# Later attention rounds in groups of 32 queries: block transposes on VectorE and small transfers in place of TensorE transposes

## The chip, the cores and the metric

The kernel runs on one core of a Trainium2 chip. The metric is device time in microseconds (us) of one execution, the median over runs. Engines are named as the profile names them: PE is TensorE (PEld its weight loads), DVE VectorE, ACT ScalarE, POOL GpSimd, SP SyncE, which here only issues transfers (DMA).

## The reference

Causal attention over 4 batches, 8 heads, 576 positions of 64 numbers, then a dense MLP on 2304 tokens, then a top-1 mixture of eight experts, all in float32:

```
rel = pos[:, None] - pos[None, :]
mask_local   = (rel >= 0) & (rel < 32)                       # heads 0..3
mask_strided = (rel >= 0) & (pos[None, :] % 32 == pos[:, None] % 32)   # heads 4..7
scores = where(mask, q @ k.T / 8, -1e9);  scores -= scores.max(-1)
attn = exp(scores); attn = attn / (attn.sum(-1) + 1e-9);  x = attn @ v       # (2304, 512)
r = maximum(x @ w_in, 0);  x = (s * r * r + b) @ w_out       # 512 -> 2048 -> 512
e = argmax(x @ w_gate)     # the token's expert: out = gate * relu(x @ w1[e]) @ w2[e]
```

## The kernel before

A local head's query sees the 32 keys up to itself, a strided head's query only keys of its own position modulo 32, so attention is done in small rounds and never as a 576 x 576 product. `GROUPS` lists the rounds as (kind, batch, first block, number n of blocks). A block of a local round ("L") is 64 consecutive queries against 96 keys. A strided head's keys of one residue are a class; a block of a strided round ("P", "U", "T") holds several classes side by side, "P" and "U" the first positions of a batch, "T" the rest of them, with 72 or 90 keys in a "T" block. Every round does its blocks for four heads at once: two heads in the two halves of the 128 partitions of q and k, and two more (index p) in the two halves of the output's partitions.

The MLP's two layers follow: `first_layer` (L918) and `second_layer` (L952) each issue twelve matmuls per step (three passes of four), for units of 256 or 512 tokens, and between them ACT squares the hidden values and splits them in two parts (L866, L878, L890), DVE takes the second part (L892). A unit's first layer needs the attention output of its tokens.

The order on every engine is written ahead by a planner, the class `Order`: each piece of work is a generator that yields (engine, cost, what it waits for), and the planner gives each engine the piece that can start first by its own estimates. What it gives is static: an engine does its instructions in that order and waits where one is not ready. The first nine rounds (`NEARLY`) run before the MLP and are not touched. The 21 later ones are spread over the MLP's steps; `PACE` names the step before which a round's scores may not stand.

A late round does this, by line: scores on PE into two banks (L585), mask added on DVE (L602), maximum (L611), difference (L625), exponential on ACT (L629), sum (L631), reciprocal (L633, L634), product (L636), all on DVE; PE transposes the probabilities by identity matmuls into PSUM (L656), ACT or DVE copies them to the buffer `ph` (L662, L664); PE multiplies with the values (L695, the PV step); ACT and DVE write the result in two parts into the MLP's input `xsl` (L734, L751). q with k, and v, come by one load each on SP's queue (L538).

Of the kernel before, what the change touches and what calls it, by code (L numbers as in the profile page):

```python
# [43 lines left out]
NEG = -8589934592.0  # L44
NQV = 2
NG = 2
# [5 lines left out]
NPR = 2  # L52
NPH = 1
NQE = 6
# [18 lines left out]
P_ATT1 = -0.1  # L73
P_ATT2 = -0.02
XLO_PE = ()
EXPB = (0, 1, 3, 4, 5, 6, 7, 8)
MASKV = range(9, 30)
# [13 lines left out]
def steps():  # L91
# [11 lines left out]


def part_of(g):

    kind, b = GROUPS[g][0:2]
    late = kind == "T"
    return FIRST[b] * late, CLS if late else FIRST[b], RES[b][late]


def dims(g):

    if GROUPS[g][0] == "L":
        return QB, LK
    j0, j1, r = part_of(g)
    return r * (j1 - j0), QB if GROUPS[g][0] == "P" else r * j1

# [9 lines left out]
def residues(g, i):  # L128
    r = part_of(g)[2]
    return range((GROUPS[g][2] + i) * r, min(STRIDE, (GROUPS[g][2] + i + 1) * r))  # L130
# [176 lines left out]
def body(ctx, tc, qkv, w12, moe_s, moe_b, wg, e12, out):  # L307
# [24 lines left out]
    m_loc0, m_loc = mk[:, 0:LK], mk[:, LK:2 * LK]  # L332
    xm = at.tile([P, max(sum(x) for x in MB[1:])], F32R, name="xm", tag="xm", bufs=1)
    mh = wp.tile([P, sum(MB[0])], F32R, name="mh", tag="w")
# [152 lines left out]
    ev_mp = Ev()  # L487
    ev_md = [Ev() for _ in range(B)]

    def masks(b, mf=None):  # L490
        if b == 0:
            yield op(("POOL", 3.0))
            make_masks(0, (1,), mf[:, 2 * LK:])
            nc.gpsimd.memset(wgt, 0.0)
            nc.gpsimd.iota(wt, pattern=[[-1, E]], base=E, channel_multiplier=0, allow_small_or_imprecise_dtypes=True)
            yield op(("ACT", 0.3))
            nc.scalar.activation(out=mh[:, MB[0][0]:], in_=mf[:, 2 * LK + MB[0][0]:], func=AF.Copy)
            o.set(ev_mb[0])
# [5 lines left out]
        nc.scalar.activation(out=xm[:, 0:sum(MB[b])], in_=t[:, 0:sum(MB[b])], func=AF.Copy)
        o.set(ev_mb[b])
        if b + 1 < B:
            o.spawn(masks(b + 1))

# [19 lines left out]
    def load_qkv(at):  # L528
        g, k = LOADS[at]
        w = widths(g)[k]  # L530
        yield op(("DMA", 0.00128 * w + (1.2 if at == 2 else 0.0)), waits=([t_qe if g < NEARLY else t_qv] if k == 0 else []) + ([t_w] if g < NEARLY else []),
                 late=LATE_Q[at] if at < len(LATE_Q) else P_QKL)
        if g < NEARLY:
            t = wp.tile([P, w], F32, name="qkv", tag="w")
        else:
            t = at_pool.tile([P, (WQ, WV)[k]], F32, name="qkv", tag=("qk", "vv")[k], bufs=NQV)[:, 0:w]
        wq = widths(g)[0]
        nc.sync.dma_start(out=t, in_=qkv[g, k * P * wq:P * (wq + k * w)].rearrange("(p n) -> p n", n=w))  # L538
        qkvs[g, k] = t
        o.set(ev_qkv[g, k], o.fin + DMA_LAT)  # L540
        if at + 1 < len(LOADS):
            o.spawn(load_qkv(at + 1), after=False)

    def attn(g):
        kind, b, i0, n = GROUPS[g]
        strided = kind == "P"
        early = g < NEARLY
        qw, w = dims(g)
        m_g = mask_of(g)
        nk = P if strided else w  # L550
        local = kind == "L"
        pairs = pair_early if early else pair_late
        singles = t_att + t_l2 if early else t_att

        def buf(name):
            if early:
                return wp.tile([P, 1024], F32, name=name, tag="w"), t_w
            return at.tile([P, {"pr": 6 * LK, "ph": 6 * P}[name]], F32, name=name, tag=name, bufs={"pr": NPR, "ph": NPH}[name]), {"pr": t_pr, "ph": t_ph}[name]

        step = PACE.get(g, -1)  # L560
        pace = [ev_k[step]] if step >= 0 else []
        yield op(("PE", n * (0.24 + 0.0015 * w) + 0.1 - (0.45 if g in MASKV else 0)), waits=[pairs, ev_qkv[g, 0], ev_mk if local else ev_mp if g < NFIRST else ev_mb[b], t_sm, t_w if early else t_pr] + pace, dep=False)
        toks = o.got[0:2]
# [17 lines left out]
        for i in range(n):  # L581
            at_i = 2 * (i % (n // 2)) + i // (n // 2) if strided else i
            for p in range(2):
                for h in range(2):
                    nc.tensor.matmul(out=sc[p * QB:(p + 1) * QB, h, at_i, :], lhsT=q[h * D:(h + 1) * D, p, i * qs:i * qs + QB],  # L585
                                     rhs=k[h * D:(h + 1) * D, p, i * kstep:i * kstep + w], start=not by_pe, stop=not by_pe or i == n - 1)
        if by_pe and g == T_LAST[b]:
            if b == 0:
                o.free(t_w)
            o.set(ev_md[b])  # L590
        if g + 1 < len(GROUPS):
# [4 lines left out]
        bc = [x.rearrange("p (h i) -> p h i", h=2).unsqueeze(3).to_broadcast([P, 2, n, w]) for x in v]  # L596
        src = sc
        if not by_pe:
            yield op(("DVE", cols / 960 + 0.15), on=toks)
            for i, j, mask in [(0, 1, m_loc0)] * a + [(a, n, m_g)] * (a < n):  # L600
                mask = (mask if mask.dtype == F32 else mask.bitcast(F32)).unsqueeze(1).unsqueeze(1).to_broadcast([P, 2, j - i, w])
                nc.vector.tensor_tensor(out=pr[:, :, i:j, :], in0=sc[:, :, i:j, :], in1=mask, op=ALU.add)  # L602
            for tok in toks:
                o.free(tok)
            src = pr
            if g == T_LAST[b]:
                if b == 0:
                    o.free(t_w)
                o.set(ev_md[b])
        yield op(("DVE", cols / 960 + 0.16), on=toks if by_pe else [])  # L610
        nc.vector.tensor_reduce(out=v[0].rearrange("p (h i) -> p h i", h=2), in_=src, axis=AX.X, op=ALU.max)  # L611
        if g in EXPB:
# [62 lines left out]
        for i in range(n):  # L675
            if not nq[i]:
                continue
            for p in range(2):
                for h in range(2):
# [14 lines left out]
                    else:  # L694
                        nc.tensor.matmul(out=dst, lhsT=lhs, rhs=rhs)  # L695
        if early:
            o.free(t_qe)
            o.free(t_w)
            o.free(t_w)
        else:  # L700
            o.free(t_qv)
        o.free(ph_tok)
# [17 lines left out]
        for k, (tok, nn, src, dst, done) in enumerate(runs):  # L720
# [1205 lines left out]
```

## Time and profile before

| | |
|---|---|
| median of 3 runs | 698.48 us (696.97 to 700.14) |
| the profiled execution | 700.7 us, span 699.0 us |
| granted TensorE clock, mean over the span | 0.992 of full speed |
| busy share of PE, DVE, ACT, POOL | 98%, 52%, 43%, 4% |
| attention's instructions on PE from 75 to 377 us (scores, transposes, PV) | 400, 98, 400 records |

The span is the profiled execution from its first to its last instruction; the 1.7 us more are what lies around it. A share is busy time over the whole span and mixes stages; which engine sets the pace of a stage is read in windows of time.

### The profile page before, as it was taken

What the parts mean: (1) busy time and instruction counts of PE and PEld (TensorE: products, weight loads), DVE (VectorE), ACT (ScalarE), POOL (GpSimd) and SP (SyncE); (2) the same over time, 40 slices, a digit from 0 to 9 for tenths busy, and PEclk for the clock granted to TensorE, in tenths of its full rate; (3) what the DMA queues carried; (4) which work ended last, traced back from release to release, by engine and by line L of the source; (5) the groups of instructions that cost most, each with busy time, mean ns of one, the idle gap of its engine ahead of it and who ended that gap; (6) DMA issues with size and microseconds to landing.
All of it is one profiled execution on the core that took longest, in us unless ns stands there. A gap on an engine that the chain in (4) does not pass through costs nothing. (4 is left out here: it accounts for less than half of the span.)

```text
span 699.0 us, 11984 instructions
## 1 busy us (share of the span) xinstructions
PE 688.2 (98%) x4702; PEld 577.3 (83%) x4702; DVE 364.5 (52%) x856; ACT 301.7 (43%) x630; POOL 25.2 (4%) x100
## 2 busy tenths in 40 slices
PE   7999999999999999999999999999999999999996
PEld 6888877898778777878778878888899999998895
DVE  4798888855144343145333144443567854764340
ACT  4776654655353443353433354554431432323221
POOL 5000000032000000000000000001000000000000
PEclk9799999999999999999999999999999999999999
DMA  8983513242222113022110023110120271307101
GB/s 303 406 315 105 198 62 114 92 145 80 91 93 69 39 40 102 1 93 72 39 46 1 0 93 123 56 62 30 61 91 1 84 255 63 120 2 265 58 10 64
DMA packets 28109, 69.00 MB, mean 99 GB/s; under 512 B 4237, under 2 KB 7310, under 8 KB 27282
## 3 DMA queue, kind: packets, MB, share of 16 engines
q1 hardware_dynamic: 27922, 68.19, 28.0%
q8 instruction: 38, 0.62, 0.4%
q14 instruction: 21, 0.17, 0.1%
q0 software_dynamic: 128, 0.02, 0.0%
HBM read 56.75 MB, written 11.69 MB: 98 GB/s over the span
## 5 line engine op out<-in xcount | busy, mean ns | idle before, releaser
L918 PE MATMUL h<-xsl,w 128*128 128x512 f32 (+1 forms) x876 | 206.8, 381 | 0.0
L952 PE MATMUL bk<-g,w 128*128 128x512 f32 (+1 forms) x864 | 203.4, 381 | 0.0
L918 PEld LDWEIGHTS h<-xsl,w 128*128 128x128 f32 x876 | 155.6, 188 | 31.4 <-issue 0.8
L952 PEld LDWEIGHTS bk<-g,w 128*128 128x128 f32 x864 | 153.3, 188 | 31.6 <-issue 2.1
L866 ACT ACTIVATE r<-h 128x512 f32<-128x512 f32 (+1 forms) x80 | 44.5, 556 | 180.8 <-PE h L918 168.4
L892 DVE TENSOR_TENSOR g<-r,g 128x512 fp32r<-128x512 f32 (+1 forms) x73 | 48.1, 659 | 131.1 <-ACT g L890 130.6
L1423 PE MATMUL bk<-w,ht 128*128 128x512 f32 x384 | 96.8, 393 | 0.0
L1423 PEld LDWEIGHTS bk<-w,ht 128*128 128x128 f32 x384 | 68.6, 188 | 12.1
L890 ACT ACTIVATE g<-r 128x512 fp32r<-128x512 f32 (+1 forms) x73 | 44.2, 605 | 2.7
L878 ACT ACTIVATE r<-r 128x512 f32<-128x512 f32 (+1 forms) x72 | 43.8, 608 | 2.2
L1316 ACT ACTIVATE ht<-h 128x256 fp32r<-128x256 f32 x24 | 9.2, 385 | 74.3 <-PE h L1477 54.5
L695 PEld LDWEIGHTS bk<-ph,qkv 96*64 96x64 f32 (+4 forms) x608 | 20.7, 144 | 9.4 <-issue 6.7
L1477 PEld LDWEIGHTS h<-x,wa 128*128 128x128 f32 x192 | 26.4, 188 | 2.3 <-issue 0.4
L1477 PE MATMUL h<-x,wa 128*128 128x256 f32 x192 | 28.0, 281 | 0.0
L1477 PE MATMUL bk<-x,wc 128*128 128x256 f32 x192 | 27.8, 280 | 0.0
L1477 PE MATMUL h<-x,wc 128*128 128x256 f32 x192 | 27.7, 280 | 0.0
L1477 PEld LDWEIGHTS h<-x,wc 128*128 128x128 f32 x192 | 25.6, 188 | 1.3 <-DVE su L1354 0.3
L1477 PEld LDWEIGHTS bk<-x,wc 128*128 128x128 f32 x192 | 24.8, 188 | 0.2 <-issue 0.2
L695 PE MATMUL bk<-ph,qkv 96*64 96x64 f32 (+9 forms) x608 | 24.6, 233 | 0.1
L585 PEld LDWEIGHTS bk<-qkv 64*64 64x64 f32 x608 | 14.2, 141 | 11.9 <-issue 6.0
L662 ACT ACTIVATE ph<-bk 96x768 f32<-96x768 f32 (+10 forms) x27 | 18.4, 680 | 12.4 <-PE bk L656 11.6
L585 PE MATMUL bk<-qkv 64*64 64x96 f32 (+4 forms) x608 | 19.8, 258 | 3.5 <-DMA qkv<-qkv 3.5
(229 smaller groups left out, 761.5 us busy)
## 6 DMA issues: line engine op xcount, KB each, us to landing
raw<-w SPq DMA_DIRECT2D x32, 512.0 KB, 7.6
qkv<-qkv SPq DMA_DIRECT2D x14, 384.0 KB, 3.2
out<-ob SPq DMA_DIRECT2D x17, 256.0 KB, 2.0
xd<-x SPq DMA_DIRECT2D x4, 1024.0 KB, 4.2
wraw<-e SPq DMA_DIRECT2D x16, 256.0 KB, 2.7
xr<-xd SPq DMA_DIRECT2D x8, 512.0 KB, 5.0
X<-xd SPq DMA_DIRECT2D x4, 1024.0 KB, 10.2
we<-e SPq DMA_DIRECT2D x8, 512.0 KB, 6.7
```

What stands on the lines that cost most here:

```text
L585: nc.tensor.matmul(out=sc[p * QB:(p + 1) * QB, h, at_i, :], lhsT=q[h * D:(h + 1) * D, p, i * qs:i * qs + QB], rhs=k[h * D:(h + 1) * D, p, ...
L662: nc.scalar.activation(out=dst, in_=pt[0:nk], func=AF.Copy)
L695: nc.tensor.matmul(out=dst, lhsT=lhs, rhs=rhs)
L866: nc.scalar.activation(out=r, in_=h, func=AF.Relu)
L878: nc.scalar.activation(out=to, in_=r, func=AF.Square)
L890: nc.scalar.activation(out=gt[:, 0, 0:U], in_=r, func=AF.Copy)
L892: nc.vector.tensor_sub(out=gt[:, 1, 0:U], in0=r, in1=gt[:, 0, 0:U].bitcast(F32))
L918: nc.tensor.matmul(out=h, lhsT=w_t[2 * fc][:, a, c * P:(c + 1) * P], rhs=xt(u, c, x), start=(c == 0 and n == 0), stop=(c == KD - 1 and n = ...
L952: nc.tensor.matmul(out=acc[pu][c], lhsT=w_t[2 * pf + 1][:, a, c * P:(c + 1) * P], rhs=gt[:, x, 0:cols(pu)], start=(first and n == 0), stop ...
L1316: nc.scalar.activation(out=ht[:, 0, a:b], in_=src, func=AF.Relu)
L1423: nc.tensor.matmul(out=acc2[s, t][0], lhsT=box[k][:, x, t * P:(t + 1) * P], rhs=w_t["p", 2 * f + 1][:, a, :], start=(f == 0 and n == 0), s ...
L1477: nc.tensor.matmul(out=banks[to], lhsT=t[:, a, off + c * P:off + (c + 1) * P], rhs=x2[s, b][:, y, c, :], start=(first and c == 0 and n == ...
```

## The change

The 21 late rounds become 14, run by a new function `attn_late`. A four-block round now covers eight tiles of 32 queries per head: 32 queries with 64 keys for a local head; two classes side by side (36 keys) for a "T" block, four to sixteen for a "P" one (32 keys). A score matmul takes 64 rows and 32 columns of the array. The probabilities lie in 32 x 32 blocks, four tiles on the four quarters of the partitions; DVE transposes all of them in one instruction (L834), and eight transfers on SP (four where there are at most 32 keys), 32 KB each, carry the blocks to the partitions at which the PV matmul wants them (L842). PV then contracts over all 128 partitions (two tiles' keys one above the other, zeros between). PE's transposes and the evictions behind them are gone. q with k and v have one buffer each instead of two; the masks are made once, on POOL; `PACE` is written anew. Its core:

```
-PACE = dict(zip(range(9, 30), (12, 14, 16, 18, 21, 24, 26, 32, 34, 36, 38, 40, 41, 42, 43, 48, 50, 52, 54, 56, 58)))
+PACE = dict(zip(range(9, 23), (12, 14, 17, 20, 24, 32, 34, 36, 39, 42, 48, 51, 54, 57)))
...
+          ("L", 1, 3, 4), ("T", 1, 0, 4), ("T", 1, 4, 4), ("L", 1, 7, 4), ("P", 2, 0, 2),
+          ("L", 2, 2, 4), ("L", 2, 6, 4), ("T", 2, 0, 4), ("T", 2, 4, 4), ("P", 3, 0, 1),
+          ("L", 3, 1, 4), ("T", 3, 0, 4), ("T", 3, 4, 4), ("L", 3, 5, 4)]
...
+    def attn_late(g):
...
+        m = 2 * n
+        cols = m * w
...
+        yield op(("PE", n * 0.1 + 0.15), waits=[pair_late, ev_qkv[g, 0], ev_ml, t_sm, t_p] + ([ev_k[PACE[g]]] if g in PACE else []), dep=False)
...
+        for i in range(n):
+            for p in range(2):
+                for x in range(2):
+                    for h in range(2):
+                        a, c = p * QB + x * QG, 2 * i + x
+                        nc.tensor.matmul(out=sc[a:a + QG, h, i, :], lhsT=q[h * D:(h + 1) * D, p, c * nq:c * nq + QG],
+                                         rhs=k[h * D:(h + 1) * D, p, c * (QG if local else w):c * (QG if local else w) + w])
...
+        yield op(("DVE", nb * m * QG / 960 + 0.15), waits=[t_pt])
+        nc.vector.transpose(out=prt[:, 0:nb * m * QG].rearrange("p (b c q) -> p b c q", b=nb, q=QG),
+                            in_=pr[:, 0:m * 2 * QG].rearrange("p (c b q) -> p b c q", b=2, q=QG)[:, 0:nb])
+        o.free(t_p)
+        yield op(("DMA", 0.4 * nb), waits=[t_ph])
+        for x in range(2):
+            for y in range(nb):
+                for p in range(2):
+                    a, r = p * QB + x * QG, x * QB + y * QG
+                    nc.sync.dma_start(out=phs[r:r + QG, p, x, 0:m * QG], in_=prt[a:a + QG, y * m * QG:(y + 1) * m * QG])
+        t1 = o.fin + DMA_LAT
...
+        yield op(("PE", 0.16 * n + 0.15), waits=[t_att, ev, ev_qkv[g, 1]] + deps)
...
+                    nc.tensor.matmul(out=og[h * D:(h + 1) * D, p * tot + 2 * i * nq:p * tot + 2 * (i + 1) * nq], lhsT=vv[:, i, p, h, :],
+                                     rhs=phs[:, p, :, c:c + nq])
```

`DMA_LAT` is 1.8: the planner books 0.8 us for a round's eight transfers and 1.8 for their landing. The mask, maximum, difference, exponential, sum, reciprocal and product stand in `attn_late` as before (L815 to L830), the two output parts at L875 and L879; the MLP's lines become L1039, L1073 and L1013.

On PE, in the middle of the MLP, one strided round's transposes and PV before, and the next round's scores:

```order
L918 MATMUL h<-xsl,w 128x512 x12
L952 MATMUL bk_856<-g,w 128x512 x3
L952 MATMUL bk_857<-g,w 128x512 x3
L656 MATMUL bk_2734<-mk,pr 72x128 x6
L952 MATMUL bk_858<-g,w 128x512 x3
L952 MATMUL bk_859<-g,w 128x512 x3
L695 MATMUL bk_2824<-ph,qkv 64x56 x12
L918 MATMUL h<-xsl,w 128x512 x12
L585 MATMUL bk_2861<-qkv 64x72 x12
```

The same kind of round in the changed kernel, from its scores to its PV:

```order
L800 MATMUL bk_2820<-qkv 32x36 x32
L1073 MATMUL bk_930<-g,w 128x512 x3
L1073 MATMUL bk_931<-g,w 128x512 x3
L1073 MATMUL bk_932<-g,w 128x512 x3
L1073 MATMUL bk_933<-g,w 128x512 x3
L1039 MATMUL h<-xsl,w 128x512 x12
L1073 MATMUL bk_930<-g,w 128x512 x3
L1073 MATMUL bk_931<-g,w 128x512 x3
L1073 MATMUL bk_932<-g,w 128x512 x3
L1073 MATMUL bk_933<-g,w 128x512 x3
L1039 MATMUL h<-xsl,w 128x512 x6
L857 MATMUL bk_2933<-phs,qkv 64x56 x16
```

Two breaks into the MLP's matmuls are left of three, and 42 of these lie between scores and PV.

On DVE, the passes of a strided round before:

```order
L602 TENSOR_TENSOR pr<-bk_3840,xm 128x432
L611 TENSOR_REDUCE sm<-pr 128x6
L892 TENSOR_TENSOR g<-r,g 128x512
L625 TENSOR_TENSOR pr<-pr,sm 128x432
L631 TENSOR_REDUCE sm<-pr 128x6
L633 TENSOR_SCALAR sm<-sm 128x6
L634 RECIPROCAL sm<-sm 128x6
L636 TENSOR_TENSOR pr<-pr,sm 128x432
```

and in the changed kernel, where the block transpose comes last:

```order
L815 TENSOR_TENSOR pr_88<-bk_2990,ml 128x8x36
L819 TENSOR_REDUCE sm<-pr_88 128x8
L821 TENSOR_TENSOR pr_88<-pr_88,sm 128x8x36
L1013 TENSOR_TENSOR g<-r,g 128x512
L825 TENSOR_REDUCE sm<-pr_88 128x8
L827 TENSOR_SCALAR sm<-sm 128x8
L828 RECIPROCAL sm<-sm 128x8
L830 TENSOR_TENSOR pr_88<-pr_88,sm 128x8x36
L834 STREAM_TRANSPOSE prt<-pr_88 128x512
```

On SP's queue, which held only loads and stores here, in the changed kernel (the blocks of two rounds, with what stands between them):

```order
L842 DMA phs<-prt 32x128 x4
L575 DMA qkv<-qkv 128x512
L575 DMA qkv<-qkv 128x1088
L575 DMA qkv<-qkv 128x1024
L1169 DMA xd_75<-x_2072 512x1x256
L1137 DMA x_2457<-xp_120 128x2048
L575 DMA qkv<-qkv 128x1088
L1169 DMA xd_76<-x_2457 128x2048
L842 DMA phs<-prt 32x256 x8
```

The eight small transfers stand behind a load of 128 x 1088 numbers and a store of 128 x 2048.

## Rows read from the trace of the kernel before

**Rows 1.** The page's first part: busy time, share of span, instructions.

```profile
PE 688.2 (98%) x4702; PEld 577.3 (83%) x4702; DVE 364.5 (52%) x856; ACT 301.7 (43%) x630; POOL 25.2 (4%) x100
```

**Rows 2.** Busy time in a window: PE, PEld, DVE, ACT, POOL; clock, DMA share, GB/s.

```profile
150.00:377.00 227.00, 227.00 (x1606) 180.98 (x1606) 90.61 (x206) 96.38 (x176) 4.36 (x20) 1.00 0.18 60
```

**Rows 3.** Waits: engine, tile, line, what for: us in total, times, longest.

```profile
ACT r L866 <- PE h L918: 168.4, 69, 4.7
DVE pr L602 <- PE bk L585: 32.2, 21, 2.7
```

**Rows 4.** PE's timeline with no round in it: start, us, matmuls.

```profile
430.27 2.88 PE L952 MATMUL bk<-g,w 128*128 128x512 f32 x12
432.99 2.88 PE L918 MATMUL h<-xsl,w 128*128 128x512 f32 x12
```

**Rows 5.** PE's timeline around a local round of three blocks.

```profile
296.03 0.73 PE L585 MATMUL bk<-qkv 64*64 64x96 f32 x24
296.69 1.66 PE L918 MATMUL h<-xsl,w 128*128 128x512 f32 x6
...
304.31 0.82 PE L656 MATMUL bk<-mk,pr 128*96 128x128 f32 x6
304.89 2.30 PE L952 MATMUL bk<-g,w 128*128 128x512 f32 x9
307.12 0.92 PE L695 MATMUL bk<-ph,qkv 96*64 96x64 f32 x24
307.97 1.06 PE L1061 MATMUL bk<-x,wgt 128*32 128x512 f32 x8
```

**Rows 6.** PE's timeline around strided rounds, the one of two blocks.

```profile
250.01 1.52 PE L918 MATMUL h<-xsl,w 128*128 128x512 f32 x6
251.46 0.48 PE L585 MATMUL bk<-qkv 64*64 64x72 f32 x16
251.87 1.64 PE L918 MATMUL h<-xsl,w 128*128 128x512 f32 x6
253.35 1.52 PE L952 MATMUL bk<-g,w 128*128 128x512 f32 x6
...
259.19 0.60 PE L656 MATMUL bk<-mk,pr 128*72 128x128 f32 x4
259.54 1.64 PE L918 MATMUL h<-xsl,w 128*128 128x512 f32 x6
261.11 0.68 PE L695 MATMUL bk<-ph,qkv 72*64 72x56 f32 x16
261.72 0.50 PE L952 MATMUL bk<-g,w 128*128 128x512 f32 x1
```

**Rows 7.** PE's timeline: scores of 64 columns, 32 records early, 16 late.

```profile
39.08 0.69 PE L585 MATMUL bk<-qkv 64*64 64x64 f32 x32
39.70 0.70 PE L914 MATMUL h<-x,wf 128*128 128x256 f32 x2
...
159.38 0.46 PE L585 MATMUL bk<-qkv 64*64 64x64 f32 x16
159.77 0.98 PE L918 MATMUL h<-xsl,w 128*128 128x256 f32 x6
```

**Rows 8.** DVE's timeline in that local round, then groups by form (count, busy, mean ns).

```profile
302.17 0.76 DVE L636 TENSOR_TENSOR pr<-pr,sm 128x576 f32<-128x576 f32 x1
...
L892 DVE TENSOR_TENSOR g<-r,g 128x512 fp32r<-128x512 f32 x42 | 29.0, 691 | 63.1 <-ACT g L890 62.7
L636 DVE TENSOR_TENSOR pr<-pr,sm 128x288 f32<-128x288 f32 x2 | 0.9, 458 | 0.1
```

**Rows 9.** SP's queue in the timeline, 257.7 to 258.7 us.

```profile
257.80 0.80 SPq L538 DMA_DIRECT2D qkv<-qkv  x2
```

**Rows 10.** DMA issues between 150 and 377 us: count, KB each, us to landing.

```profile
qkv<-qkv SPq DMA_DIRECT2D x4, 128.0 KB, 2.0
...
scd<-scl SPq DMA_DIRECT2D x1, 5.0 KB, 1.4
```

More of the change, by code (lines that the diff above doesn't have):

```diff
@@ L44 @@
 NEG = -8589934592.0
-NQV = 2
 NG = 2
@@ L52 @@
 NPR = 2
-NPH = 1
+QG = 32
 NQE = 6
@@ L73 @@
 P_ATT1 = -0.1
-P_ATT2 = -0.02
+P_ATT2 = 0.1
 XLO_PE = ()
 EXPB = (0, 1, 3, 4, 5, 6, 7, 8)
-MASKV = range(9, 30)
 P_GATE = -0.2
@@ L108, in part_of @@
     late = kind == "T"
+    if g >= NEARLY:
+        return FIRST[b] * late, CLS if late else FIRST[b], 2 if late else QG // FIRST[b]
     return FIRST[b] * late, CLS if late else FIRST[b], RES[b][late]
@@ L114, in dims @@
     if GROUPS[g][0] == "L":
-        return QB, LK
+        return (QB, LK) if g < NEARLY else (QG, 2 * QG)
     j0, j1, r = part_of(g)
+    if g >= NEARLY:
+        return r * (j1 - j0), r * j1
     return r * (j1 - j0), QB if GROUPS[g][0] == "P" else r * j1
@@ L128, in residues @@
 def residues(g, i):
-    r = part_of(g)[2]
+    r = part_of(g)[2] * (1 if g < NEARLY else 2)
     return range((GROUPS[g][2] + i) * r, min(STRIDE, (GROUPS[g][2] + i + 1) * r))
@@ L175, in widths @@
     qw, w = dims(g)
+    if g >= NEARLY:
+        return 2 * (2 * n * qw + QG - qw) + 2 * (n * QB + QG if kind == "L" else 2 * n * w), n * 2 * P
     if kind == "L":
@@ L332, in body @@
     m_loc0, m_loc = mk[:, 0:LK], mk[:, LK:2 * LK]
-    xm = at.tile([P, max(sum(x) for x in MB[1:])], F32R, name="xm", tag="xm", bufs=1)
+    xm = at.tile([P, MB[1][0]], F32R, name="xm", tag="xm", bufs=1)
+    LATE_MASKS = (("T", 1), ("P", 2), ("T", 2), ("P", 3), ("T", 3))
+    late_w = [CLS * 2 if kind == "T" else QG for kind, b in LATE_MASKS]
+    ml = at.tile([P, 4 * QG + sum(late_w)], F32, name="ml", tag="ml", bufs=1)
+    late_m = {x: ml[:, 4 * QG + sum(late_w[:k]):4 * QG + sum(late_w[:k + 1])] for k, x in enumerate(LATE_MASKS)}
+    prs = [at.tile([P, 1024 // 2], F32, name=f"pr{k}", tag=f"pr{k}", bufs=1) for k in range(NPR)]
+    prt = at.tile([P, 1024 // 2], F32, name="prt", tag="prt", bufs=1)
+    phs = at.tile([P, 2, 2, 256], F32, name="phs", tag="phs", bufs=1)
     mh = wp.tile([P, sum(MB[0])], F32R, name="mh", tag="w")
@@ L432, in body @@
         open_banks(k, pair_early[k], True)
-    t_qe, t_qv, t_pr, t_ph = Tok(NQE), Tok(NQV), Tok(NPR), Tok(NPH)
+    t_qe, t_qk, t_vv, t_pt, t_ph = Tok(NQE), Tok(1), Tok(1), Tok(1), Tok(1)
+    t_pr = [Tok(1) for _ in range(NPR)]
     t_sm = Tok(NSM)
@@ L487, in body @@
     ev_mp = Ev()
-    ev_md = [Ev() for _ in range(B)]
     def masks(b, mf=None):
@@ L499, in masks, with masks_late @@
             return
-        yield op(("POOL", 8.0), waits=[ev_k[0]] if b == 1 else [ev_md[b - 1]])
-        t = at_pool.tile([P, sum(MB[1])], F32, name="xt", tag="xt", bufs=1)
-        make_masks(b, (0, 1), t)
+        yield op(("POOL", 8.0), waits=[ev_k[0]])
+        t = at_pool.tile([P, MB[1][0]], F32, name="xt", tag="xt", bufs=1)
+        make_masks(1, (0,), t)
         yield op(("ACT", 0.35))
[L504 to L507, printed above, removed]
+        nc.scalar.activation(out=xm, in_=t, func=AF.Copy)
+        o.set(ev_mb[1])
+        o.spawn(masks_late())
+    ev_ml = Ev()
+    def masks_late():
+        yield op(("POOL", 4.5))
+        for t in prs + [phs]:
+            nc.gpsimd.memset(t, 0.0)
+        loc = ml[:, 0:4 * QG].rearrange("p (i k) -> p i k", i=2)
+        nc.gpsimd.memset(loc, 0.0)
+        for a in range(0, P, QG):
+            x = loc[a:a + QG]
+            nc.gpsimd.affine_select(out=x, in_=x, pattern=[[0, 2], [-1, 2 * QG]], compare_op=ALU.is_ge, fill=NEG, base=STRIDE, channel_multiplier=1)
+            nc.gpsimd.affine_select(out=x, in_=x, pattern=[[0, 2], [1, 2 * QG]], compare_op=ALU.is_gt, fill=NEG, base=0, channel_multiplier=-1)
+            if a % QB == 0:
+                nc.gpsimd.memset(x[:, 1, 0:STRIDE], NEG)
+        for kind, b in LATE_MASKS:
+            yield op(("POOL", 5.0))
+            j0, j1 = (FIRST[b], CLS) if kind == "T" else (0, FIRST[b])
+            v, nj = late_m[kind, b], j1 - j0
+            r = v.shape[1] // j1
+            nc.gpsimd.memset(v, 0.0)
+            for a in range(0, P, QG):
+                x = v[a:a + QG].rearrange("p (r j) -> p r j", j=j1)
+                for pattern, base, sign in (([[-nj, r], [-1, j1]], j0, 1), ([[nj, r], [0, j1]], nj - 1, -1)) + ((([[-nj, r], [0, j1]], 0, 1),) if j0 else ()):
+                    nc.gpsimd.affine_select(out=x, in_=x, pattern=pattern, compare_op=ALU.is_ge, fill=NEG, base=base, channel_multiplier=sign)
+        o.set(ev_ml)
     ev_k = [Ev() for _ in range(NU * NF)]
@@ L530, in load_qkv @@
         w = widths(g)[k]
-        yield op(("DMA", 0.00128 * w + (1.2 if at == 2 else 0.0)), waits=([t_qe if g < NEARLY else t_qv] if k == 0 else []) + ([t_w] if g < NEARLY else []),
+        yield op(("DMA", 0.00128 * w + (1.2 if at == 2 else 0.0)), waits=([t_qe] * (k == 0) + [t_w] if g < NEARLY else [(t_qk, t_vv)[k]]),
                  late=LATE_Q[at] if at < len(LATE_Q) else P_QKL)
@@ L535, in load_qkv @@
         else:
-            t = at_pool.tile([P, (WQ, WV)[k]], F32, name="qkv", tag=("qk", "vv")[k], bufs=NQV)[:, 0:w]
+            t = at_pool.tile([P, (WQ, WV)[k]], F32, name="qkv", tag=("qk", "vv")[k], bufs=1)[:, 0:w]
         wq = widths(g)[0]
@@ L546, in attn @@
         strided = kind == "P"
-        early = g < NEARLY
+        if g >= NEARLY:
+            yield from attn_late(g)
+            return
         qw, w = dims(g)
@@ L551, in attn @@
         local = kind == "L"
-        pairs = pair_early if early else pair_late
-        singles = t_att + t_l2 if early else t_att
+        pairs = pair_early
+        singles = t_att + t_l2
         def buf(name):
[L556 to L562, printed above, removed]
+            return wp.tile([P, 1024], F32, name=name, tag="w"), t_w
+        yield op(("PE", n * (0.24 + 0.0015 * w) + 0.1), waits=[pairs, ev_qkv[g, 0], ev_mk if local else ev_mp if g < NFIRST else ev_mb[b], t_sm, t_w], dep=False)
         toks = o.got[0:2]
@@ L574, in attn @@
         a = 1 if local and not i0 else 0
-        by_pe = g not in MASKV
-        for h in range(2 if by_pe else 0):
+        for h in range(2):
             if a:
@@ L585, in attn @@
                     nc.tensor.matmul(out=sc[p * QB:(p + 1) * QB, h, at_i, :], lhsT=q[h * D:(h + 1) * D, p, i * qs:i * qs + QB],
[L586 to L590, printed above, removed]
+                                     rhs=k[h * D:(h + 1) * D, p, i * kstep:i * kstep + w], start=False, stop=i == n - 1)
+        if g == T_LAST[0]:
+            o.free(t_w)
         if g + 1 < len(GROUPS):
@@ L596, in attn @@
         bc = [x.rearrange("p (h i) -> p h i", h=2).unsqueeze(3).to_broadcast([P, 2, n, w]) for x in v]
[L597 to L611, printed above, removed]
+        yield op(("DVE", cols / 960 + 0.16), on=toks)
+        nc.vector.tensor_reduce(out=v[0].rearrange("p (h i) -> p h i", h=2), in_=sc, axis=AX.X, op=ALU.max)
         if g in EXPB:
@@ L623, in attn @@
         else:
-            yield op(("DVE", cols / 960 + 0.15), on=toks if by_pe else [])
-            nc.vector.tensor_tensor(out=pr, in0=src, in1=bc[0], op=ALU.subtract)
-            for tok in toks if by_pe else []:
+            yield op(("DVE", cols / 960 + 0.15), on=toks)
+            nc.vector.tensor_tensor(out=pr, in0=sc, in1=bc[0], op=ALU.subtract)
+            for tok in toks:
                 o.free(tok)
@@ L641, in attn @@
             nt = len(hs) * nj
-            yield op(("PE", nt * 0.09 + 0.15), waits=[some] + ([t_w if early else t_ph] if 0 in hs else []), dep=(0 in hs))
+            yield op(("PE", nt * 0.09 + 0.15), waits=[some] + ([t_w] if 0 in hs else []), dep=(0 in hs))
             toks = [t for t in o.got if t in t_att or t in t_l2]
@@ L695, in attn @@
                         nc.tensor.matmul(out=dst, lhsT=lhs, rhs=rhs)
[L696 to L701, printed above, removed]
+        o.free(t_qe)
+        o.free(t_w)
+        o.free(t_w)
         o.free(ph_tok)
@@ L753, in attn, with seen @@
                 o.free(tok)
+        seen(g)
+    def seen(g):
         for u in xuses[g]:
@@ L1872, in layout @@
         qs = QB if kind == "P" else qw
+        if g >= NEARLY:
+            nqk = 2 * (2 * n * qw + QG - qw)
+            qq = qk[:, :, 0:nqk].reshape(2, D, 2, -1)
+            kk = qk[:, :, nqk:].reshape(2, D, 2, -1)
+            vv = vv.reshape(P, n, 2, 2, D)
+            t0 = b * S + i0 * QB
+            for p in range(2):
+                for h in range(2):
+                    if kind == "L":
+                        qa, ka, va = (x[:, 2 * p + h].reshape(NT, D) for x in (q, k, v))
+                        qq[h, :, p] = qa[t0:t0 + n * QB].T
+                        kk[h, :, p] = ka[t0 - QG:t0 + n * QB].T
+                        for c in range(2 * n):
+                            vv[c % 2 * QB:c % 2 * QB + QB, c // 2, p, h] = va[t0 + (c - 1) * QG:t0 + (c + 1) * QG]
+                        continue
+                    hd = 4 + 2 * p + h
+                    j0, j1, r = part_of(g)
+                    for c in range(2 * n):
+                        rr = (2 * i0 + c) * r + np.arange(r)[:, None]
+                        qq[h, :, p, c * qw:(c + 1) * qw] = q[b, hd, (rr + STRIDE * np.arange(j0, j1)).ravel()].T
+                        tk = (rr + STRIDE * np.arange(j1)).ravel()
+                        kk[h, :, p, c * w:(c + 1) * w] = k[b, hd, tk].T
+                        vv[c % 2 * QB:c % 2 * QB + w, c // 2, p, h] = v[b, hd, tk]
+            continue
         nqk = 2 * (n * qs + QB - qs)
```

80 lines of the change are left out of this document (79 added, 1 removed), and 3 rows, old and new, of the table GROUPS.

## The prediction

> **What bounds the kernel now.** I read the page's busy line first [rows 1]: TensorE (PE) is busy for 688.2 us of 699.0, VectorE (DVE) for 52% and ScalarE (ACT) for 43%. That is an average, so I then read the stretch in which most of the changed rounds run [rows 2]: between 150 and 377 us PE is busy for 227.00 of 227.00 us at a granted clock of 1.00 (the 2.4 GHz level), while DVE is busy for 90.61 us. The list of waits [rows 3] says the same from the other side: DVE waits for the scores of the late rounds (L602 on L585), 32.2 us over 21 rounds, and ACT waits for PE far longer. So every microsecond of PE that a late round costs lengthens the end, and work of DVE, ACT or a DMA costs nothing until PE has to wait for it.
>
> **What a late round costs on PE.** The MLP's own pace is twelve 512-wide matmuls in 432.99 − 430.27 = 2.72 us [rows 4], 0.2267 each. A round breaks into it three times: scores, transposes, probabilities times values (PV). I price each from its start to the next main matmul's start, and add what the main matmuls next to it lose. Scores of a three-block local round: 296.69 − 296.03 = 0.66; its six transposes 304.89 − 304.31 = 0.58; its PV 307.97 − 307.12 = 0.85 [rows 5]. Of a two-block round: 0.41, 0.35, 0.61 [rows 6]. The neighbours: six main matmuls should take 1.36 us, but take 1.45 ahead of the scores (250.01 to 251.46), 1.48 behind them (251.87 to 253.35), and 1.57 between transposes and PV (259.54 to 261.11) [rows 6]. That is 0.09 lost ahead of a break and about 0.13 behind it, 0.22 for each of scores and PV, some 0.11 for the transposes. A three-block local round thus costs 0.88 + 0.69 + 1.07 = 2.64 us.
>
> Over 21 rounds (ten of three blocks, nine of two, two of one):
> - PV: 10 × 1.07 + 9 × 0.83 + 2 × 0.61 = 19.4 us.
> - Transposes: 10 × 0.68 + 9 × 0.46 + 2 × 0.24 = 11.4 us.
> - Scores: five local three-block rounds at 0.88; the five strided ones (72 columns, one with 90) at some 0.77; nine of two blocks at 0.63 to 0.71; two of one block at 0.49: 15.2 us.
>
> Together 46.0 us; the two rounds of one block are carried down along the line through two and three.
>
> **What it costs after.** There are 14 rounds: twelve of four blocks, one of two, one of one. Transposes leave PE: 0. The trace shows two records for each of these matmuls (the order lists 12 where it shows 24).
> - PV. The sixteen matmuls of a round make 32 records, 64 columns wide or a little less. From 16 to 24 records the price goes from 0.61 to 0.85 [rows 5, 6], 0.03 a record (0.028 through all sizes), so 32 cost 0.85 + 0.22 = 1.07, and with 0.23 beside them 1.30: 12 × 1.30 + 0.84 + 0.62 = 17.1 us.
> - Scores. No row shows a tile of 64 × 32. The nearest are 64 × 64 tiles at 64 columns: 16 records 0.39, 32 records 0.62 [rows 7], so 0.155 fixed and 0.0145 a record. PV has two tiles on the array and takes 0.028 a record; these have four and take 0.0145: the price halves as the tiles double. With eight tiles 0.007 would follow, but records then have to be issued at twice the rate shown anywhere here. The bounds are 0.0067 and 0.0145 (nothing gained by the narrow tile), with 0.028 as the far end (narrow tiles in pairs). I take 0.010 for local rounds, whose 64 columns are those of the row, and 0.0075 for the strided ones (36 columns). A four-block round is 64 records: 0.155 + 0.64 + 0.23 = 1.03 local, 0.87 strided; 6 × 1.03 + 6 × 0.87 + 0.63 + 0.51 = 12.5 us.
>
> Sum 29.6 against 46.0: **16.4 us of PE less** (18.0 at 0.0067, 11.7 at 0.0145 throughout, 0.7 at 0.028).
>
> The Trainium skill speaks against this edit: "TensorE: Matmul & The Clock Gate", section "Wait — 56ns, not 53.3ns?", says that matmuls never start closer than about 25 ns however few columns they have. By that rule 64 records cost 1.6 us and the scores an estimated 25.8 us in all, so that only some 3 us are saved. The trace bears it out at one place only, PV's 0.028; the scores' 0.0145 contradict it, so I give it little.
>
> **DVE and ACT.** Twenty-one rounds' passes become fourteen's, narrower for strided rounds (288 elements a pass instead of 432), and a block transpose of 128 × 512 is new. The order below shows it behind the normalizing multiply. No row has it; between the 0.46 us of a 288-wide pass and the 0.69 of a 512-wide one [rows 8] I take 0.70, and as the other end 2 us. DVE idles for over half of this stretch [rows 2], and ACT loses its evictions of the transposes, so neither becomes the bound: 0 on the path, except within the chain below. The late masks, built once on GpSimd, lie where it idles (4% busy [rows 1]).
>
> **The new wait.** Where PE transposed at once, eight transfers of 32 KB now go out on SP, and PV waits for the last. SP issues one in about 0.4 us: two take 0.80 [rows 9]. Landing is 1.4 us for 5 KB and 2.0 for 128 KB [rows 10], so about 1.6. The stage is 7 × 0.4 + 1.6 = 4.4 us; bounds 3.4 (issue at 0.25) and 6.4 (queued behind a neighbouring load, or landing in 3.6). Against it stands the main work that the order puts between scores and PV. The order below has one such place: behind the scores of a strided round come 12 + 12 + 12 + 6 = 42 main matmuls, 9.5 us. The chain in the profiled round takes from 296.69 (scores done) to 302.93 (multiply done) 6.2 us [rows 5, 8]. A four-block local round has 512 elements instead of 576, five passes 0.06 shorter each, so 5.9; plus transpose 0.7 and stage 4.4 makes 11.0 where nothing else intervenes, 9 to 10.9 for a strided round. Each round also has the MLP's own DVE work between its passes (0.69 each [rows 8]) and waits for ACT behind it, up to 3 us; counted round by round from the order, room against chain is 13.1/13.3, 13.5/13.0, 11.0/11.7, one ample, one 0.9 short (its only block buffer is released late by the round before), 15.9/16.0, 13.0/14.0, 9.5/8.9, 10.9/10.7, 9.5/9.0, 12.1/12.2, 11.3/10.8, 10.9/10.7, 10.9/11.2. The excesses add to 3.3 us; with handovers between engines I take **4.3 us of PE stall**. Everything behind PV on PE's in-order queue, the whole MLP, is late with it. The rounds lie so close to their room that the stage decides: 1 us more makes about 14 us of stalls, 2 us more about 24; 1 us less leaves nearly none.
>
> **Sum.** −16.4 + 4.3 = −12.1 us on the profiled execution's 700.7, which lies 2.2 above the median of 698.48: about 688.6 profiled, 686.4 as a median; I say **687 us**. A measurement of this kernel tells about 0.5%, 3.5 us, from no change.
>
> **Rivals.**
> - *The narrow tiles don't run eight at a time.* At four (0.0145) the saving is 11.7 and the time 698.5 − 11.7 + 4.3 = 691. At the pair rate, or nearly, it is 0.7 to 3 and the time 700 to 702. For it: no row shows eight tiles. Against: the price halved from two tiles to four. 0.09 for the first, 0.08 for the second.
> - *The blocks arrive late (slower).* The eight transfers share SP with loads of up to 544 KB and stores of 1 MB; the order of SP shows one of each straight ahead of a round's eight. If the stage takes 6.4 us instead of 4.4, PE stands before PV in nearly each round: −16.4 + 24 = +8, so 706. It decides from a stage of about 5.6 us, where the stalls eat the 16.4. For it: most rooms are within 1 us of their chain. Against: the DMA engines are busy for a share of only 0.18 in this stretch [rows 2]. 0.17.
> - *Saved and given back.* A block transpose of about 2 us, or a stage about 1 us too long, makes 14 to 17 us of stalls: 697 to 699, no change. 0.09.
>
> **How the numbers follow.** My forecast has 0.57, with 680 (18 saved, no stall) to 692 (9 us of stall) as its own range. Faster: 0.57 + 0.09 = 0.66. Within 0.5%: 0.08 + 0.09 = 0.17. Slower: 0.17. The range reaches over the rivals at 691 and 699 and into the pair rate, and leaves out the late blocks and what little lies below: 680 to 702.
>
> **What would show it.** In the profile after: no transposes between 75 and 380 us; a four-block score insertion of 0.64 to 0.80 us from its start to the next main matmul (1.1 would be four tiles, 1.9 pairs); PV 1.05 to 1.1; and in the list of waits PE's PV waiting for the moved blocks by 3 to 6 us in all. If that wait is 14 us or more, the stage was mis-sized and the forecast is wrong on the slow side; a wait of zero with 681 us would mean that transfers land earlier than their rows. A granted clock under 1.00 behind such waits would make me wrong in a way that no row of before shows.

## The result, and the profile after

The changed kernel takes 701.73 us (median, 699.27 to 705.25, 20 runs) against 697.49 before in the same comparison (695.93 to 701.25, 20 runs): a ratio of 1.0057, 95% interval 1.004 to 1.0073. It is slower by about 4 us, where 687 was forecast. The profiled execution of before, on which the rows ahead rest, had a slow first stretch: from 10 to 20 us its granted clock was 0.74 (1.00 in the changed kernel), and it reached the 512-wide part of the MLP at 61.78 us, the changed kernel at 58.40.

The page of the changed kernel, its busy line, and two windows of its busy time (PE, PEld, DVE, ACT, POOL; granted clock, DMA share, GB/s); they answer to [rows 1, 2]:

```profile
PE 674.9 (96%) x5028; PEld 568.6 (81%) x5028; DVE 345.7 (49%) x809; ACT 284.9 (41%) x598; POOL 39.5 (6%) x140
```

```profile
75.00:150.00 75.00, 72.30 (x680) 60.85 (x679) 55.04 (x109) 36.74 (x68) 0.72 (x12) 0.98 0.41 134
150.00:377.00 227.00, 214.39 (x1775) 172.73 (x1774) 73.47 (x160) 81.28 (x145) 0.45 (x8) 0.99 0.22 71
```

The earlier of the two windows in the kernel before, which the rows ahead don't have:

```profile
75.00:150.00 75.00, 75.00 (x547) 62.40 (x546) 61.79 (x117) 40.42 (x74) 5.64 (x22) 1.00 0.34 115
```

PE, which never idled in this stretch, now idles for 15.3 us of 302, while every engine does less. The list of waits (us in total, times, longest) names for what:

```profile
DVE pr L815 <- PE bk L800: 26.2, 14, 3.9
PEld bk L857 <- issue: 18.0, 19, 2.7
PE bk L857 <- DMA phs<-prt: 12.3, 17, 2.2
PE bk L857 <- DMA qkv<-qkv: 2.3, 1, 2.3
```

PV (L857) waits for the moved blocks, and once, in the round of two blocks, for the load of its values. (PEld's row is idle time of PV's weight loads for which the profile names no releaser.) One strided round shows it: SP's queue, then DVE, then PE in the timeline (start, us, work, idle before and what ended it):

```profile
249.52 5.18 SPq L842 DMA_DIRECT2D phs<-prt  x8
```

```profile
248.29 0.46 DVE L830 TENSOR_TENSOR pr<-pr,sm 128x288 f32<-128x288 f32 x1
248.78 0.71 DVE L834 STREAM_TRANSPOSE prt<-pr 128x512 f32<-128x512 f32 x1
```

```profile
242.39 0.77 PE L800 MATMUL bk<-qkv 64*32 64x36 f32 x64
243.09 1.67 PE L1039 MATMUL h<-xsl,w 128*128 128x512 f32 x6
...
252.78 1.52 PE L1039 MATMUL h<-xsl,w 128*128 128x512 f32 x6
255.40 0.33 PE L857 MATMUL bk<-phs,qkv 128*64 128x56 f32 x4 [1.10 <-DMA phs<-prt]
256.04 1.03 PE L857 MATMUL bk<-phs,qkv 128*64 128x56 f32 x28 [0.31 <-DMA phs<-prt]
256.99 1.19 PE L1039 MATMUL h<-xsl,w 128*128 128x512 f32 x4
```

The block transpose ends at 249.49. SP needs until 254.70 to issue eight transfers: 5.18 us, where the forecast's step of 0.4 would make it 3.1. From one issue to the next it takes 0.66 here, 0.62 in most rounds. The last lands near 256.0, 6.5 us after the transpose; the forecast had 4.4. PE stands for 1.10 us ahead of PV and 0.31 within it, until the last blocks are there. Most rounds look like this; in the rounds of four blocks the stage is 6.2 to 6.5 us where SP has nothing else ahead of it, and 7.0 and 7.4 in the two where a load stands ahead.

Waiting had a second price. Behind its two longest waits for blocks PE ran at the 1.2 GHz level for a while (granted clock 0.50). Behind one of them twelve matmuls take 4.61 us, which take 2.88 elsewhere [rows 4]:

```profile
218.39 0.34 PE L857 MATMUL bk<-phs,qkv 128*64 128x64 f32 x4 [2.16 <-DMA phs<-prt]
...
219.98 4.61 PE L1039 MATMUL h<-xsl,w 128*128 128x512 f32 x12
```

### The profile page after: what moved, and what is told of

It reads as the page before. It is cut to its first block, busy times and chain, and to the rows that moved or that the text cites. A ratio compares the mean times of both kernels' runs of the same rounds, so it can differ in the third digit from the quotient of the medians.

```text
span 700.8 us, 12794 instructions
## 1 busy us (share of the span) xinstructions
PE 674.9 (96%) x5028; PEld 568.6 (81%) x5028; DVE 345.7 (49%) x809; ACT 284.9 (41%) x598; POOL 39.5 (6%) x140
## 5 line engine op out<-in xcount | busy, mean ns | idle before, releaser
L1039 PE MATMUL h<-xsl,w 128*128 128x512 f32 (+1 forms) x876 | 207.3, 382 | 0.0
L1073 PE MATMUL bk<-g,w 128*128 128x512 f32 (+1 forms) x864 | 198.8, 378 | 0.0
L1039 PEld LDWEIGHTS h<-xsl,w 128*128 128x128 f32 x876 | 157.2, 189 | 31.5 <-issue 0.8
L1073 PEld LDWEIGHTS bk<-g,w 128*128 128x128 f32 x864 | 155.4, 189 | 32.2 <-issue 1.3
L1013 DVE TENSOR_TENSOR g<-r,g 128x512 fp32r<-128x512 f32 (+1 forms) x73 | 48.1, 659 | 156.1 <-ACT g L1011 155.9
L1544 PEld LDWEIGHTS bk<-w,ht 128*128 128x128 f32 x384 | 68.6, 188 | 12.2
L857 PE MATMUL bk<-phs,qkv 128*64 128x64 f32 (+2 forms) x408 | 17.9, 232 | 15.3 <-DMA phs<-prt 12.3
L857 PEld LDWEIGHTS bk<-phs,qkv 128*64 128x64 f32 x408 | 15.1, 143 | 21.4 <-issue 18.0
L879 DVE TENSOR_TENSOR xsl<-bk,xsl 128x512 fp32r<-128x512 f32 (+4 forms) x14 | 8.6, 613 | 35.5 <-ACT xsl L875 35.5
L875 ACT ACTIVATE xsl<-bk 128x512 fp32r<-128x512 f32 (+4 forms) x14 | 7.5, 535 | 43.1 <-PE bk L857 43.0
L815 DVE TENSOR_TENSOR pr<-bk,ml 128x288 f32<-128x288 f32 (+5 forms) x17 | 7.6, 462 | 26.2 <-PE bk L800 26.2
## 6 DMA issues: line engine op xcount, KB each, us to landing
out<-ob SPq DMA_DIRECT2D x17, 256.0 KB, 3.2
wraw<-e SPq DMA_DIRECT2D x16, 256.0 KB, 2.7
```

The lines of the kernel that those rows point to most:

```text
L815: nc.vector.tensor_tensor(out=ps4[:, :, i:j], in0=sc[:, :, i:j], in1=mask.unsqueeze(1).unsqueeze(1).to_broadcast([P, 2, j - i, w]), op=ALU ...
L857: nc.tensor.matmul(out=og[h * D:(h + 1) * D, p * tot + 2 * i * nq:p * tot + 2 * (i + 1) * nq], lhsT=vv[:, i, p, h, :], rhs=phs[:, p, :, c: ...
L879: nc.vector.tensor_sub(out=dst[1], in0=src, in1=dst[0].bitcast(F32))
L1013: nc.vector.tensor_sub(out=gt[:, 1, 0:U], in0=r, in1=gt[:, 0, 0:U].bitcast(F32))
L1039: nc.tensor.matmul(out=h, lhsT=w_t[2 * fc][:, a, c * P:(c + 1) * P], rhs=xt(u, c, x), start=(c == 0 and n == 0), stop=(c == KD - 1 and n = ...
L1073: nc.tensor.matmul(out=acc[pu][c], lhsT=w_t[2 * pf + 1][:, a, c * P:(c + 1) * P], rhs=gt[:, x, 0:cols(pu)], start=(first and n == 0), stop ...
```

## The experiments

Each starts from the changed kernel. Two theories stood against each other: that SP's issues, 0.62 us each, make PE wait before PV, by what the stage exceeds the planner's booking; or that the loss lies elsewhere (landing, the single buffers of v, q with k and the blocks, DVE, a slower PE after standing).

**Half the transfers.**

```
-                for p in range(2):
+                for p in range(1):
                     a, r = p * QB + x * QG, x * QB + y * QG
                     nc.sync.dma_start(out=phs[r:r + QG, p, x, 0:m * QG], ...)
```

> Leaves out half of the block transfers (those of the second pair of heads, whose output is then wrong); the order of all else is that of the changed kernel. Theory (SP's issues are the cost): each of the eight transfers holds SP for 0.62 us instead of 0.4, so the stage is 7 x 0.62 + 1.85 = 6.2 us; with four it is 3 x 0.62 + 1.85 = 3.7, PV finds its blocks in nearly every round, PE's 19 us of waiting before and inside PV fall to 1 to 3, and the time to 684 to 688. Rival (a transfer's landing, the one buffer of v and of the blocks, or a slow PE after it stood idle is the cost, not the number of issues): stage near 6, time 698 to 702.

Measured: 683.46 us, ratio 0.9808 (0.9791 to 0.9824). Other values of attention could change how many tokens each expert gets, but the part behind the MLP is as long as in the changed kernel (211.9 and 211.4 us). With the same order on every engine, four issues less a round (two where there were four) are worth 18 us. The window of the late rounds is nearly full again:

```profile
150.00:377.00 227.00, 225.64 (x1794) 182.28 (x1793) 73.61 (x154) 85.89 (x150) 0.26 (x4) 1.00 0.20 65
```

**Twice as many transfers of half the size.**

```
+                    for c in range(2):
+                        c0, c1 = c * m * QG // 2, (c + 1) * m * QG // 2
+                        nc.sync.dma_start(out=phs[r:r + QG, p, x, c0:c1], in_=prt[a:a + QG, y * m * QG + c0:y * m * QG + c1])
```

> Each block transfer is cut in two of half its columns: sixteen a round, the same bytes; the order of all else is that of the changed kernel. Theory (the count of SP's issues is the cost): the pitch stays at 0.62 us, the stage grows to 15 x 0.62 + 1.85 = 11.2 us, PE stands some 4 to 5 us longer in each of twelve rounds, time 750 to 765. Rival (bytes, or the landing of each transfer, are the cost): pitch near 0.31, stage near 6.5, time 700 to 706.

Measured: 788.2 us in a single run, more than either theory said. The stage is 11.2 to 11.4 us where nothing stands ahead, and the step from issue to issue 0.63: between 16 and 32 KB the bytes don't matter, the count does, and that part fell as forecast. The DMA issues from 150 to 377 us (count, KB each, us to landing), ahead for the changed kernel and then for this one:

```profile
phs<-prt SPq DMA_DIRECT2D x71, 32.0 KB, 1.8
```

```profile
phs<-prt SPq DMA_DIRECT2D x96, 16.0 KB, 1.8
```

The excess is the clock, as far as the trace tells. In the MLP PE idles 59.7 us instead of 15.3, nearly the 4 us a round that were forecast; the MLP's matmuls between the breaks take 21 us more, though they are the same. PE's timeline and the window around it:

```profile
270.05 1.52 PE L1041 MATMUL h<-xsl,w 128*128 128x512 f32 x6
275.36 0.29 PE L859 MATMUL bk<-phs,qkv 128*64 128x56 f32 x2 [3.79 <-DMA phs<-prt]
...
278.89 2.93 PE L1041 MATMUL h<-xsl,w 128*128 128x512 f32 x6
```

```profile
150.00:300.00 150.00, 129.93 (x1051) 106.81 (x1048) 47.93 (x101) 48.31 (x92) 1.04 (x16) 0.88 0.22 74
```

After standing 3.79 us, PE takes 2.93 us for six matmuls that took 1.52 ahead of it: the 1.2 GHz level. The mean granted clock of the window is 0.88. My estimate had added up the waits alone.

**The planner books what the transfers take.** Nothing but one number is edited:

```
-        yield op(("DMA", 0.4 * nb), waits=[t_ph])
+        yield op(("DMA", 2.2 * nb), waits=[t_ph])
```

> The planner books 4.4 us for a round's eight transfers instead of 0.8, what they take; nothing else is edited, so it sets PV later. Theory: the stage stays at 6.2 us, but PV stands behind 3 to 4 us more of the MLP's work, PE's waits before PV fall from 19 us to under 4, time 685 to 690. Rival (one buffer of v, of the blocks and of q with k): a later PV delays the next round's loads and blocks, the wait moves there or to the next unit's first layer, 695 to 702.

Measured: 681.2 us, ratio 0.9784 (0.9757 to 0.981). By the order, PV now stands behind 13.6 to 15 us of the MLP's matmuls in most rounds instead of 9.5 to 12.3. Its two windows and a round on PE, with the same eight transfers on SP:

```profile
75.00:150.00 75.00, 75.00 (x752) 64.18 (x751) 57.42 (x116) 38.59 (x74) 0.91 (x14) 1.00 0.42 138
150.00:377.00 227.00, 226.57 (x1798) 183.25 (x1797) 73.85 (x155) 86.21 (x152) 0.26 (x4) 1.00 0.22 70
```

```profile
236.22 5.19 SPq L842 DMA_DIRECT2D phs<-prt  x8
```

```profile
242.49 1.52 PE L1073 MATMUL bk<-g,w 128*128 128x512 f32 x6
243.94 1.15 PE L857 MATMUL bk<-phs,qkv 128*64 128x56 f32 x32
245.01 1.19 PE L1073 MATMUL bk<-g,w 128*128 128x512 f32 x4
```

The transfers are as slow as they were, and PE no longer notices: it idles for 0.43 us in the whole stretch. The single buffers cost no more than that here; in the changed kernel they cost the one wait of 2.3 us, where a round's blocks had to wait for their buffer and the load of its values stood behind them on SP. A dose between, 1.1 * nb (2.2 us for a full round):

> A dose between: the planner books 2.2 us for a round's eight transfers (0.8 in the changed kernel, 4.4 in the one that took the stalls away). Between scores and PV the MLP's work grows by 1.3 us in most rounds, 2.7 in a few. Theory (PE's loss is what the 6.2 us stage exceeds the booked one by): of 19 us of waits some 3 to 6 stay, time 684 to 688. Rival (any later PV helps by freeing something else): 681 to 682, as with the full price.

Measured: 686.51 us, 0.9846 (0.9829 to 0.9864). Counted from the last MLP matmul ahead of each PV to the first one behind it (without the gate's matmuls, which stand there in two rounds), PV's breaks take 4.9 us more than with the full booking; in the changed kernel they take 18.6 more. Price and loss go together.

**Scores earlier.**

```
-PACE = dict(zip(range(9, 23), (12, 14, 17, 20, 24, 32, 34, 36, 39, 42, 48, 51, 54, 57)))
+PACE = dict(zip(range(9, 23), (12, 13, 16, 19, 23, 31, 33, 35, 38, 41, 47, 50, 53, 56)))
```

> The changed kernel with each late round but the first allowed to begin its scores one MLP step earlier (PACE less 1), all else as it is. If the planner still sets PV by its booked 0.8 us, PV moves ahead with the scores, the distance stays and so do the stalls: 698 to 703. If other waits hold PV where it was, the distance grows by up to 5.4 us, the stalls vanish and the time is 682 to 688. By the theory the booked price and not the scores' place is at fault, so the first.

Measured: 711.21 us, 1.0199 (1.0159 to 1.0238): no gain, as the theory said, but 8 us worse than its range. PV did move ahead with the scores; in the first two rounds its distance shrank from 12.2 to 10.9 us, in the sixth from 13.6 to 10.9. PV's breaks take some 4 us more than in the changed kernel, the MLP's matmuls between them some 2.5 more, with the granted clock at 0.98 in the windows from 60 to 150 and from 150 to 377 us. That one step of `PACE` does so much was not foreseen, and not followed further. With the full booking added:

> Scores one step earlier, which alone made the kernel slower still (711 us), now with the planner booking 4.4 us for the transfers. Theory: what made it slow is PV's distance from its scores, not the scores' place; with the distance right (13 to 17 us), no stall stays and the time is 681 to 684. Rival (earlier scores themselves hold up units or loads): 688 to 695.

Measured: 680.77 us, 0.9762 (0.9742 to 0.9781), no different from the booking alone by more than the intervals. Earlier scores cost nothing once PV's distance is right.

**Another way to issue, and no transfers at all.** Half of them on ACT's queue:

```
+                    (nc.sync, nc.scalar)[p].dma_start(out=phs[r:r + QG, p, x, 0:m * QG], ...)
```

> Four of a round's eight transfers are issued by ACT instead of SP. Theory (SP's issues): four issues a queue, stage 3.7 to 4 us, PE's waits before PV fall from 19 us to under 5 and the time to 685 to 690. Rival 1 (the two queues share what makes an issue slow): pitch doubles, stage stays near 6, time 700. Rival 2 (2.4 us of issues on ACT delay the MLP's squares): PE then waits for the second layer's input, 692 to 700.

Measured: 685.56 us, 0.9834 (0.9818 to 0.9851). This doesn't separate the two causes as I meant it to: the planner books 2.4 us on ACT, so PV stands later too (13.6 us in most rounds), and ACT issues its four only behind the MLP's squares, so the stage of a four-block round is 5.9 to 9 us, hardly shorter in any round and longer in some. The time is close to the 686.5 of 2.2 us booked with all eight on SP, so the booking alone can account for it. It shows that ACT's issues have the same step, 0.61 to 0.64 us in all rounds but one.

DVE moving the blocks itself:

```
+                    nc.vector.transpose(out=phs[r:r + QG, p, x, 0:m * QG].rearrange("p (c q) -> p c q", q=QG), in_=prv[a:a + QG, y])
```

> No transfers: DVE transposes eight pieces of 32 x 256 straight to the partitions where PV reads them, eight instructions of some 0.42 us (3.4 us in all) in place of one of 0.71 us and a stage of 6.2. Theory: blocks are there 3.5 us earlier, PE's waits before PV go from 19 us to under 3, time 683 to 688. Rival (DVE's 3.4 us hold up the MLP's L1013, or PE's loss has another cause than the transfers): 693 to 702.

Measured: 688.53 us, 0.9877 (0.9861 to 0.9894). The waits for blocks are gone, but not the loss at one place: between 126 and 136 us PE waits for a PV and then for a unit's input, with matmuls that the planner fills such holes with (L1953). The second lot of these ran at the 1.2 GHz level, twelve in 2.93 us against nineteen in 2.43. An instruction of 32 x 256 took 0.44 us.

```profile
126.33 2.43 PE L1953 MATMUL bk<-xsl 128*128 128x256 f32 x19
130.28 1.45 PE L853 MATMUL bk<-phs,qkv 128*64 128x48 f32 x32 [1.52 <-issue]
132.96 2.93 PE L1953 MATMUL bk<-xsl 128*128 128x256 f32 x12 [1.23 <-DVE xsl L875]
```

With the second and third late round's scores set earlier (`PACE` 13 and 15 for 14 and 17):

> The kernel without transfers (DVE moves the blocks in eight transposes), with the second and third late round's scores one and two steps earlier. In the one without this, PE lost some 8 us at a single place, 126 to 136 us, where a round's PV and then a unit's input were late. Expected: that loss goes, others stay at nothing, 680 to 683. Rival: DVE's eight pieces hold up the MLP's own passes there, 686 to 690.

Measured: 684.34 us, 0.9818 (0.9778 to 0.9857): about 4 us of that loss went; the unit's input is still late there, and the time is above what I expected. It beats the kernel before, and not the booking.

**What makes an issue slow.** Transfers of 128 partitions instead of 32:

```
-                    nc.sync.dma_start(out=phs[r:r + QG, p, x, 0:m * QG], in_=prt[a:a + QG, y * m * QG:(y + 1) * m * QG])
+                    nc.sync.dma_start(out=phs[:, p, x, 0:m * QG], in_=prt[:, y * m * QG:(y + 1) * m * QG])
```

> Eight transfers a round, each of 128 partitions instead of 32 and as many columns (128 KB, four times the bytes): they move the wrong blocks, so late attention's output is wrong; order unchanged. It asks what makes an issue slow. Theory 1 (any transfer from and to the chip's own memory): pitch stays 0.62, stage 6.2 to 6.8, time 702 to 708. Theory 2 (the narrow shape of 32 partitions): pitch 0.40 to 0.47 as the loads of 128 partitions have, stage 5.0 to 5.6 with a landing of 2.0 to 2.5, time 690 to 697.

Measured: the time, 848.4 us in a single run, says nothing here: what it moves changes the experts' shares, and behind the MLP PE waits 82.1 us for expert weights. The stage does: an issue takes 0.49 us instead of 0.59, but the step is 0.84 on average where SP has nothing else ahead, and the stage 7.8 to 8.8 us. Five of the seven steps are 0.51 to 0.69, near those of the narrow transfers, and two are pauses of some 1.45. Neither theory fits the whole; the narrow shape is not what makes the steps long, and what does is left open.

## Why the prediction was wrong

**The terms on PE held.** From the first 512-wide MLP matmul to the start of what follows the last, the kernel before takes 487.39 − 61.78 = 425.6 us, the changed one 489.43 − 58.40 = 431.0, the one with the right booking 467.97 − 58.01 = 410.0 (between the first two that is 5.4 us; the medians differ by 4.2). The lines, in pairs for the three kernels:

```profile
61.78 1.04 PE L918 MATMUL h<-xsl,w 128*128 128x512 f32 x3
487.39 0.86 PE L1452 MATMUL h<-x,wa 128*128 128x256 f32 x6
58.40 1.27 PE L1039 MATMUL h<-xsl,w 128*128 128x512 f32 x4
489.43 0.75 PE L1573 MATMUL h<-x,wa 128*128 128x256 f32 x5
58.01 1.28 PE L1039 MATMUL h<-xsl,w 128*128 128x512 f32 x4
467.97 0.75 PE L1573 MATMUL h<-x,wa 128*128 128x256 f32 x5
```

Where PV finds its blocks, the change is worth 15.6 us; the sum said 16.4. Its parts, too: a four-block strided round's scores take 243.09 − 242.39 = 0.70 us to the next main matmul, a local one's, in PE's timeline of the changed kernel,

```profile
296.35 0.86 PE L800 MATMUL bk<-qkv 64*32 64x64 f32 x64
297.14 1.67 PE L1039 MATMUL h<-xsl,w 128*128 128x512 f32 x6
```

0.79 (0.64 to 0.80 was forecast), and PV without a wait takes 245.01 − 243.94 = 1.07, the forecast 1.07. So the first rival, narrow tiles that don't run side by side, did not come about: 64 records in 0.79 us with everything fixed in it is 12 ns each, against the floor of some 25 ns that the Trainium skill gives in "TensorE: Matmul & The Clock Gate", section "Wait — 56ns, not 53.3ns?". With eight tiles the floor doesn't show here; PV's 28 ns a record, with two, would allow for it.

**DVE held.** The block transpose takes 0.71 us (0.70 was taken), and with 49% DVE is less busy than before.

**The step that failed** is "SP issues one in about 0.4 us: two take 0.80 [rows 9]". It made a price for eight small transfers within the chip from two large loads. The block transfers are slower to issue from the start: two of them, of only 8 KB, take 1.15 us where the two loads took 0.80 (from the run with half the transfers):

```profile
254.94 1.15 SPq L842 DMA_DIRECT2D phs<-prt  x2
```

In a run of eight the step is 0.62, 1.5 us more for seven steps, and landing is 1.8 instead of 1.6 [rows 10]; the stage is 6.2 to 6.5 us where I had 4.4. The trace of before had issues as slow, of other and larger transfers in SP's queue behind the MLP, four in a row in 3.05 us, 0.62 to 0.74 apart:

```profile
565.62 3.05 SPq L1716 DMA_DIRECT2D X<-xd  x4
```

I had taken 6.4 us as the far bound and given it 0.17. With the rooms as close as the count had them, that term decides everything: 21.1 us (431.0 − 410.0) of PE go to it instead of 4.3, 18.6 of them at PV's breaks (1.10 + 0.31 us of visible waiting in the round shown), the rest in MLP matmuls, some of which ran at the 1.2 GHz level behind a wait (mean granted clock 0.98 and 0.99 in the two windows). Of the signs that the prediction named, the granted clock under 1.00 came; the wait for blocks stands in the list with 12.3 us, twice the forecast and yet short of the 14 that were to mean a mis-sized stage, since a list of waits holds only a part of what the breaks lose. That 701.7 still lies in the stated 680 to 702 is luck: the range reached that far for narrow tiles that don't run side by side, and these ran as forecast.

**The rival that came about** is the second, "the blocks arrive late", in its outcome: the stage at its 6.4, PE standing before PV in most rounds. Its price was 24 us and 706 us; it measured 21 and 701.7. Its cause was another: it had the transfers queued behind a load, or landing in 3.6 us. A load stood ahead in two rounds only, and a landing took 1.8 us; the issues themselves were slow. The experiments exclude the alternatives as far as they go: with the order of everything kept, half of the issues bring 18 us back and twice as many lose 87; with the issues kept, a later PV brings 20 back, so buffers (but for the one wait of 2.3 us), DVE and landing are not what holds PE. That the late blocks come from issue count is shown; why one issue in a row takes 0.6 us is not.

## What to carry to other kernels

Where work moves off the engine that sets the pace, its new way round has to be priced in latency, from a row of the same kind of transfer, with as many issues in a row as the change will make, and set against the work that the order puts between producer and consumer. A planner that writes a static order makes a wrong price visible as waits on the bounding engine: correcting that one number (0.4 * nb to 2.2 * nb here) turned a kernel 0.6% slower than before into one 2.2% faster, with the same instructions in another order. When many rounds sit within 1 us of their room, the uncertain term of the stage should set the forecast's width, since an error in it counts once for each round.

## What the runs showed of the hardware

- Small transfers within the chip, on one queue, were issued 0.62 to 0.63 us apart in runs of eight or sixteen, whether they carried 16 or 32 KB; on ACT's queue 0.61 to 0.64. Single loads of up to 544 KB were issued in 0.33.
- Eight-way use of the array: 64 x 32 tiles gave 64 records in 0.70 us at 36 columns and 0.79 at 64, against 0.62 for 32 records on four tiles [rows 7].
- DVE wrote a 32 x 32 block transpose to another quarter of the partitions in 0.44 us for 32 x 256 numbers, which takes the place of a transfer where DVE has time.
- After a wait of 3.79 us (twice as many transfers) PE's next matmuls ran at the 1.2 GHz level. In the changed kernel they did so after waits of 1.98 and 2.16 us, not after one of 2.30 nor after those of 1.4 us or less; these two stretches are why its windows show 0.98 and 0.99.
